# A fused attention and MLP kernel on one core: v's large part is loaded late, four waits are reordered, and the quotients are spread wider

## The chip, the cores and the metric

The kernel runs on one core of a Trainium2 chip. The metric is the device time of one execution in microseconds (us), the median of three runs. A profile of one execution goes with it. Engines are named as in the profile: PE multiplies matrices (PEld is its weight loading), DVE, ACT and POOL work element by element, SP issues the transfers (DMAs).

## The reference

There are 2048 tokens of 640 numbers each. One layernorm feeds two branches, and x is added to both:

```python
xn = layernorm(x)
return x + A(xn) + B(xn)

# A: linear attention, 32 heads of 20
q, k, v = split(xn @ wqkv)
phi(p) = concat(softmax(p @ w_phi), softmax(-(p @ w_phi)))   # per head, 20 -> 40 features
kv, z  = phi(k)^T v, sum over tokens of phi(k)
o      = phi(q) kv / (phi(q) z + 1e-6)                       # the quotient
A      = o @ wo

# B: MLP, 640 -> 1728 -> 640
B = gelu(xn @ w1 + b1) @ w2 + b2
```

## The kernel before, in words

Everything is float32. The kernel cuts each factor into a hi part, which PE's faster format holds exactly, and a lo part, the rest. Each product is three matmuls: hi by hi (line L70), hi by lo (L71), lo by hi (L72). Hi parts are cut by ACT (L61), lo parts by DVE or POOL (L64). PE's instructions are put in the order of the code by hand (`manual_schedule`). The other engines' orders come from a scheduler, which is held at some places by `issue_after`. Waits come from tiles and from the eight PSUM banks.

The work has three phases.

**Phase 1** (0 to 222 us) is the MLP for token blocks 0 and 1 (a block is 512 tokens). `mlp.passes(g, b)` takes two chunks of 128 hidden units: a first layer (`first`, then `gelu` at L260, then the split of the hidden tile m), and a second layer of five output pieces, each of which DVE adds to `acc` (L305). PE needs the bank that an L305 frees two pieces later. All that must be ready for phase 2 is made beside the MLP by the generator `prep()`, which is advanced once per three matmuls, about 0.68 us: the k and q weights are multiplied with `w_phi` (`prep_fold`: PE L460, then ACT L61 and DVE L64 out of the bank into `wkh` and `wkl`; a fold of q has two parts, so two hi and two lo), layernorm statistics, v's weights (`load_v`), and the normalised blocks 2 and 3 (`raw` is loaded, L532 on POOL subtracts, L535 on DVE multiplies, L539 on ACT and L542 on DVE split, and both parts go to DRAM). v's weights have a small part (128 columns), which goes into `wkh`/`wkl`, and a large part (512 columns), which is split in `prep()`, stored in DRAM as `wv_dram`, and read back at the start of phase 2 into the weight slots w2 and w3 (L584 to L588).

**Phase 2** (222.7 to 439 us) goes over 16 tiles of 128 tokens. `proj(t, i)` computes one of four column parts of a tile with 15 matmuls, i = 3 being v's large part. `k_tile` and `q_tile` make the features: maxima on DVE (L629, L630), differences on POOL (L640), the exponential on ACT (L641), sums on DVE (L643), quotients on POOL (L651, or L694 and L696). `kv_tile` multiplies k's features of a tile with its v, in ten matmuls L675 into banks that accumulate and one matmul L679 into the next bank in turn. `ptile` hands out banks 0, 1 and 2 in turn. `TAIL` lists the order of the last eight projections by hand.

**Phase 3** (439 to 731 us) is the MLP for blocks 2 and 3. Beside it run the last two `kv_tile`s (`last_kv`), and then `attend()`: for each block, groups of features are read from DRAM into `e`, split (ACT L893, POOL L894) and multiplied with kv (PE L900, L901), and `quotients()` divides (`ob`): it spreads the reciprocals `rx` over the partitions, one DVE shuffle (L944) and one POOL multiplication (L946) for each of five column chunks. At the end comes the output projection: `split` (L963, L965) and additions at L1068.

Of the kernel before, what the change touches and what calls it, by code (L numbers as in the profile page):

```python
# [15 lines left out]
P = 128  # L16
# [35 lines left out]
def tile_kernel(ctx: ExitStack, tc: tile.TileContext, x, xT, wkT, wqT, wv, wphi, wo, w1, b1, w2, b2,  # L52
# [33 lines left out]

    e_dram = [tc.dram_tile([2 * D, 512], F32, name=f"e{b}") for b in range(NB)]
    y_dram = [[tc.dram_tile([P, KC, 512], F32, name=f"y{p}{b}") for p in "hl"] for b in range(2)]
    wv_dram = [tc.dram_tile([P, KC, VF * H], F32, name=f"wv{p}") for p in "hl"]
    wo_dram = [tc.dram_tile([P, KC, D], F32, name=f"wo{p}") for p in "hl"]  # L90
    o_dram = [tc.dram_tile([2 * DH, 512], F32, name=f"o{b}") for b in range(NB)]
    r_dram = tc.dram_tile([2, 8, P], F32, name="r")
# [359 lines left out]
    def prep_fold(n, g, raw):  # L452

        kk, kd = (G6, G5) if g < 5 else (2 * DH, 2 * DF)
        parts = [(0, 0, DF)] if n == "k" else [(KQ, 0, B1F), (C3, B1F, DF)]

        for k, ni in ((0, 4), (4, 1)):
            ps = mlp.px()
            for i in range(ni):
                nc.tensor.matmul(ps[:, i * kd:(i + 1) * kd], raw[:kk, (k + i) * P:(k + i + 1) * P],  # L460
                                 wpt[:kk, g, :kd // DF, 1:], start=True, stop=True)
            for c, f0, f1 in parts:
                hi, lo = (w[:, k:k + ni, c:c + (f1 - f0) * H].rearrange("p i (f h) -> p i h f", h=H)[:, :, 6 * g:6 * g + kd // DF]
                          for w in wkv_)
                split(hi, lo, ps[:, :ni * kd].rearrange("p (i h f) -> p i h f", i=ni, f=DF)[:, :, :, f0:f1])
            for _ in range(3):
                yield

# [15 lines left out]
    def prep():  # L484
        jobs = [(n, g) for n in "kq" for g in range(6)]
        ahead = raws(*jobs[0])
        for _ in range(2):
            yield
        nc.vector.tensor_tensor(wpt[:, :, :, 1:], wpt[:, :, :, 1:], wpt[:, :, :, 0:1].to_broadcast([G6, 6, 6, DF]), op=ALU.subtract)
        more = more_stats()  # L490
        for i, job in enumerate(jobs):
            raw = ahead
            ahead = raws(*jobs[i + 1]) if i < 11 else None
            for k, _ in enumerate(prep_fold(*job, raw)):
                if i > 0 and k % 3 == 1:
                    next(more, None)
                yield

        def load_v(kc):
            raw = fp.tile([P, D], F32, name="raw")  # L500
            nc.sync.dma_start(raw, wv[kc * P:(kc + 1) * P, :])
            return raw

        for _ in more:
            yield
        ahead = load_v(0)
        mr = load_rows(2)
        for kc in range(KC):
            raw, ahead = ahead, load_v(kc + 1) if kc < KC - 1 else None
            for _ in range(5):  # L510
                yield
            split(*[w[:, kc, C2:C3] for w in wkv_], raw[:, VF * H:])
            t = fp.tile([P, 2, KC, G5], F32R, name="t").rearrange("p a c f -> p a (c f)")[:, :, :VF * H]
            split(t[:, 0], t[:, 1], raw[:, :VF * H])
            for p in range(2):
                nc.sync.dma_start(wv_dram[p][:, kc, :], f(t[:, p]))


        def load(b, c):
            xc = fp.tile([P, D], F32, name="raw")[:, :512]  # L520
            nc.sync.dma_start(xc, xT[c * P:(c + 1) * P, b * 512:(b + 1) * 512])
            return xc

        for b in range(2, 4):
            ahead = load(b, 0)
            if b == 3:
                mr = load_rows(3)
            for _ in range(5 if b == 2 else 10):
                yield
            for c in range(KC):  # L530
                xc, ahead = ahead, load(b, c + 1) if c < KC - 1 else None
                nc.gpsimd.tensor_tensor(xc, xc, mr[:, 0], op=ALU.subtract)  # L532
                for _ in range(3):
                    yield
                nc.vector.tensor_tensor(xc, xc, mr[:, 1], op=ALU.mult)  # L535
                for _ in range(2):
                    yield
                hl = fp.tile([P, 2, KC, G5], F32R, name="t").rearrange("p a c f -> p a (c f)")[:, :, :512]
                nc.scalar.activation(hl[:, 0], xc, AF.Copy)  # L539
                for _ in range(2):  # L540
                    yield
                nc.vector.tensor_tensor(hl[:, 1], xc, f(hl[:, 0]), op=ALU.subtract)  # L542
                for p in range(2):
                    nc.sync.dma_start(y_dram[b - 2][p][:, c, :], f(hl[:, p]))
                yield

    mlp.beside = prep()
    p11 = mlp.passes(1, 1, [wc[2], wc[3]])
    next(p11)
# [7 lines left out]
    for g in range(2, 7):  # L557
        for b in range(2):
            if b == 0:
                ws, wn = wn, []  # L560
            this = mlp.passes(g, b, ws)
            next(this)
            finish(before)
            before = this
            if g < 6:
                wn.append(mlp.take(2 * g + 2 + b))
            if 2 * g + b < 11:
                mlp.fetch(2 * g + 3 + b)
    finish(mlp.beside)
    finish(before)  # L570
    rs.close()
    order.close()
    for b in range(2):
# [9 lines left out]
    wv_ = [wp.tile([P, 4, D], F32R, name=f"w{2 + p}").rearrange("p i d -> p (i d)").rearrange("p (c d) -> p c d", c=KC)
           for p in range(2)]  # L584
    for p in range(2):
        nc.sync.dma_start(f(wv_[p]), wv_dram[p])
# [11 lines left out]
    def proj(t, i):  # L598
# [2 lines left out]
        c = slice((t % 4) * P, (t % 4) * P + P)  # L601
        wh, wl = [w[:, :, slice(*CB[i])] for w in wkv_] if i < 3 else wv_
        ps = ptile()[:, :wh.shape[2]]
        for kc in range(KC):
            mm3(ps, yh[:, kc, c], yl[:, kc, c], wh[:, kc], wl[:, kc], kc == 0, kc == KC - 1)
        return ps

    turn, exps, subs = [0], {}, {}
# [99 lines left out]
            nc.sync.dma_start(ed[q], ets[b][n][32 * q:32 * q + 32])  # L708

    fts, ets = {}, {}  # L710
    TAIL = [(14, 0), (14, 1), (15, 0), (15, 1), (14, 2), (14, 3), (15, 3), (15, 2)]
    places = [acc01.tile([P, KC, 512], F32, name=f"acc{n}").rearrange("p c (j n) -> p (c j) n", n=P) for n in range(2)]
    places = [p[:, j:j + 10] for p in places for j in (0, 10)] + [et.tile([P, 10, P], F32, name="et")]

# [1 line left out]
    for t, i in [(t, i) for t in range(14) for i in range(4)] + TAIL:  # L716
# [19 lines left out]
        else:  # L736
            evac = v_parts(t, ps, 0)

        tk = 13 if (t, i) == (15, 1) else t - 2 if 1 < t < 15 and i == 0 else None
        if tk is not None:  # L740
            kv_tile(tk, fts.pop(tk), vbuf[tk % 2])
        if i == 0 and t in (1, 2, 3, 6, 7):
# [7 lines left out]
            for w, wd in zip((f(hi), lo), wo_dram):  # L750
                nc.sync.dma_start(wd[:, kc, :], w)
        if (t, i) == (11, 0):
            mlp = Mlp((0, 2, 3, 1), ((1, 2), (0, 3)))
            mlp.ph = ptile
            mlp.fetch(0)
        if (t, i) == (12, 3):
# [93 lines left out]
    class Attention:  # L850
# [65 lines left out]
        def quotients(self):  # L916
# [25 lines left out]
            for c in range(KC + 1):  # L942
                if c < KC:
                    nc.vector.stream_shuffle(rx[:, c, :], rx[:, c, :], SPREAD)  # L944
                if c:
                    nc.gpsimd.tensor_tensor(ob[:, c - 1, :], ob[:, c - 1, :], rx[:, c - 1, :], op=ALU.mult)  # L946
# [185 lines left out]
```

## Time and profile before

| | us |
|---|---|
| three runs | 730.85, 732.10, 732.47 (median 732.1) |
| profiled execution | 732.27, its span 730.5 |
| PE busy | 719.0 (98% of the span), 3440 matmuls |
| DVE, POOL, ACT busy | 478.3, 371.3, 328.7 |

A row of the profile's timeline gives the start, the duration, the engine, the line of the kernel, the operation, the tiles it writes and reads, and in brackets how long the engine had been idle and what it waited for. The PE works almost without a break, so the question at each place is whether PE waits there and for whom. Idle time of another engine costs nothing in itself.

### The profile page before, as it was taken

To read this page: it belongs to the slowest core of one execution; us is meant where nothing else is said; L and a number is where in the kernel's file an instruction comes from. 1 tells how busy PE (TensorE), PEld (TensorE's weight loads), DVE (VectorE), ACT (ScalarE), POOL (GpSimd) and SP (SyncE) were. 2 spreads that over 40 slices of the span, in tenths; PEclk is the share of its full clock that TensorE was granted. 3 is DMA by queue.
4 is the path that set the end of the run, shared out by engine and by line. 5 is a ranking of instruction groups with operands and counts; after the bars stand their busy time and mean duration, and the time that the engine had idled before them with its cause. 6 is when DMAs were issued, how large, how long until landed. Compare 5 with 4: busy or idle time off the path is not lost.

```text
span 730.5 us, 9719 instructions
## 1 busy us (share of the span) xinstructions
PE 719.0 (98%) x3440; PEld 601.6 (82%) x3440; DVE 478.3 (65%) x796; ACT 328.7 (45%) x542; POOL 371.3 (51%) x322
## 2 busy tenths in 40 slices
PE   9999999999999999999999998999999999999998
PEld 7788878878888888888888887888878878887887
DVE  7837655466754788788898787435575656766431
ACT  7624554442423545545445546246565556530110
POOL 2211122234232997897878879346586777404000
PEclk9999999999999999999999999999999999999999
DMA  9704425754562127236302405934443453163222
GB/s 324 218 19 142 145 77 177 223 188 153 166 214 118 72 91 231 76 109 202 88 1 55 126 1 186 244 128 123 131 127 116 127 159 97 49 227 121 81 84 75
DMA packets 60016, 96.59 MB, mean 132 GB/s; under 512 B 7016, under 2 KB 28920, under 8 KB 58344
## 3 DMA queue, kind: packets, MB, share of 16 engines
q1 hardware_dynamic: 59680, 95.97, 42.0%
q8 instruction: 27, 0.44, 0.3%
q14 instruction: 21, 0.17, 0.1%
q10 hardware_dynamic: 288, 0.01, 0.0%
HBM read 65.61 MB, written 30.35 MB: 131 GB/s over the span
## 4 chain that ended last, share of the span: by engine, by line
PE 79%; DVE 8%; ACT 4%; DMA 3%; POOL 3%; issue 2%; SPq 0%; POOLq 0%; DVEq 0%; ACTq 0%
PE bank L70 24%; PE bank L71 23%; PE bank L72 23%; PE bank L675 2%; PE bank L460 2%; DVE rx L944 1%; DVE m L64 1%; POOL e L894 1%; PE bank L901 1%; DVE st L136 1%; PE bank L900 1%; DMA raw<-in_wv 1%; DVE y L965 1%; POOL w L64 1%; ACT m L260 1%
## 5 line engine op out<-in xcount | busy, mean ns | idle before, releaser
L64 POOL TENSOR_TENSOR w<-r,w 128x640 fp32r<-128x640 f32 x52 | 83.0, 1616 | 125.2 <-ACT w L61 96.0
L70 PE MATMUL bank<-y,w 128*128 128x512 f32 (+1 forms) x334 | 131.7, 394 | 0.4 <-DVE ob L1068 0.4
L71 PE MATMUL bank<-y,w 128*128 128x512 f32 (+1 forms) x334 | 129.9, 389 | 0.0
L72 PE MATMUL bank<-y,w 128*128 128x512 f32 (+1 forms) x334 | 129.8, 389 | 0.0
L70 PE MATMUL bank<-m,w 128*128 128x512 f32 x260 | 103.9, 400 | 3.5 <-DVE acc L305 2.5
L72 PE MATMUL bank<-m,w 128*128 128x512 f32 x260 | 101.5, 390 | 0.0
L71 PE MATMUL bank<-m,w 128*128 128x512 f32 x260 | 101.3, 390 | 0.0
L305 DVE TENSOR_TENSOR acc<-bank,acc 128x512 f32<-128x512 f32 x120 | 80.9, 683 | 16.8 <-PE bank L72 9.0
L70 PE MATMUL bank<-wkh,y 128*128 128x512 f32 (+1 forms) x240 | 87.7, 366 | 0.0
L71 PE MATMUL bank<-wkl,y 128*128 128x512 f32 (+1 forms) x240 | 87.4, 364 | 0.0
L72 PE MATMUL bank<-wkh,y 128*128 128x512 f32 (+1 forms) x240 | 87.0, 363 | 0.0
L64 DVE TENSOR_TENSOR m<-m,m 128x512 fp32r<-128x512 f32 (+1 forms) x54 | 42.6, 788 | 59.7 <-ACT m L61 59.7
L70 PEld LDWEIGHTS bank<-y,w 128*128 128x128 f32 x334 | 63.1, 189 | 13.4 <-DVE ob L1068 0.8
L72 PEld LDWEIGHTS bank<-y,w 128*128 128x128 f32 x334 | 63.2, 189 | 13.2
L71 PEld LDWEIGHTS bank<-y,w 128*128 128x128 f32 x334 | 63.2, 189 | 12.2
L641 ACT ACTIVATE m<-m,rs_all 128x1280 f32<-128x1280 f32 x32 | 43.7, 1365 | 42.6 <-POOL m L640 42.5
L70 PEld LDWEIGHTS bank<-m,w 128*128 128x128 f32 x260 | 48.9, 188 | 16.0 <-DVE acc L305 5.1
L643 DVE TENSOR_REDUCE sm<-m 128x64 f32<-128x1280 f32 x32 | 47.4, 1482 | 17.2 <-ACT m L641 17.0
L894 POOL TENSOR_TENSOR e<-e,m 128x512 fp32r<-128x512 f32 x28 | 38.1, 1361 | 40.1 <-ACT m L893 35.4
L72 PEld LDWEIGHTS bank<-m,w 128*128 128x128 f32 x260 | 48.8, 188 | 10.3
L71 PEld LDWEIGHTS bank<-m,w 128*128 128x128 f32 x260 | 48.9, 188 | 9.3
L260 ACT ACTIVATE m<-bank,b1t 128x512 f32<-128x512 f32 (+1 forms) x54 | 36.1, 670 | 44.7 <-PE bank L72 40.7
(156 smaller groups left out, 1395.5 us busy)
## 6 DMA issues: line engine op xcount, KB each, us to landing
r<-in_w SPq DMA_DIRECT2D x52, 320.0 KB
e<-e SPq DMA_DIRECT2D x40, 256.0 KB
e<-acc SPq DMA_DIRECT2D x52, 160.0 KB
acc<-in_xT SPq DMA_DIRECT2D x4, 1280.0 KB
xb<-in_x SPq DMA_DIRECT2D x8, 320.0 KB
t<-in_x SPq DMA_DIRECT2D x8, 320.0 KB
raw<-in_xT SPq DMA_DIRECT2D x10, 256.0 KB
yh<-t SPq DMA_DIRECT2D x10, 256.0 KB
```

The source lines that it names most:

```text
L64: eng.tensor_tensor(lo, src, f(hi), op=ALU.subtract)
L70: nc.tensor.matmul(ps, lh, rh, start=first, stop=False, **kw)
L71: nc.tensor.matmul(ps, lh, rl, start=False, stop=False, **kw)
L72: nc.tensor.matmul(ps, ll, rh, start=False, stop=last, **kw)
L136: nc.vector.bn_stats(st[:, i, h, :], xb[:, h * 320:(h + 1) * 320])
L260: nc.scalar.activation(gt, pz, AF.Gelu_apprx_tanh, bias=b1t[:, 2 * g + j:2 * g + j + 1])
L305: nc.vector.tensor_tensor(acc[b][:, m, :], pw, acc[b][:, m, :], op=ALU.add)
L460: nc.tensor.matmul(ps[:, i * kd:(i + 1) * kd], raw[:kk, (k + i) * P:(k + i + 1) * P], wpt[:kk, g, :kd // DF, 1:], start=True, stop=True)
L641: exps[n, t] = nc.scalar.activation(e, e, AF.Exp, scale=rs_all[:, t:t + 1])
L643: nc.vector.tensor_reduce(sm, e.rearrange("p s (h f) -> p (s h) f", f=DH), axis=AX, op=ALU.add)
L675: nc.tensor.matmul(kvp[g // 2][:, (g % 2) * 240:(g % 2) * 240 + 240].rearrange("p (s f) -> p s f", s=4), v[:, g * VS:(g + 1) * VS], ft[:, ...
L894: nc.gpsimd.tensor_tensor(pl, e, f(ph), op=ALU.subtract)
```

## The change

1. `wv_dram` is gone. `prep()` loads v's small part alone, with one strided DMA, and splits it once; eight steps of the generator stand where 25 stood. So the normalised blocks 2 and 3, which follow, are made 17 steps earlier. SP issues five loads of 320 KB, ten stores of 256 KB and two reads of 1280 KB less. The large part is loaded by `load_v` at pass (6, 0), five DMAs of 256 KB, and split by `split_v` straight into the slots w2 (hi, ACT) and w3 (lo, POOL) beside the second layer of that pass.
2. `prep_fold` issues both hi parts of a fold before both lo parts.
3. The last two projections change places: (15, 2) now comes before (15, 3). For i = 3, that is v's large part, in all 16 tiles, the five products hi by lo come first, then hi by hi and lo by hi in turn. `kv_tile(14)` comes right after (15, 3) and no longer inside the first layer of phase 3. The second MLP takes its weight slots in the order 0, 3, 2, 1, and `load_wo` uses w2 and w1.
4. `quotients()` leaves three steps between column chunks and no longer two.

```diff
@@ prep_fold
-            for c, f0, f1 in parts:
-                hi, lo = (w[:, k:k + ni, c:c + (f1 - f0) * H].rearrange("p i (f h) -> p i h f", h=H)[:, :, 6 * g:6 * g + kd // DF]
-                          for w in wkv_)
-                split(hi, lo, ps[:, :ni * kd].rearrange("p (i h f) -> p i h f", i=ni, f=DF)[:, :, :, f0:f1])
+            ops = [...]
+            for src, hi, lo in ops:
+                nc.scalar.activation(hi, src, AF.Copy)
+            for src, hi, lo in ops:
+                nc.vector.tensor_tensor(lo, src, f(hi), op=ALU.subtract)
@@ prep
-        ahead = load_v(0)
         mr = load_rows(2)
-        for kc in range(KC):
-            raw, ahead = ahead, load_v(kc + 1) if kc < KC - 1 else None
-            for _ in range(5):
-                yield
-            split(*[w[:, kc, C2:C3] for w in wkv_], raw[:, VF * H:])
-            t = fp.tile([P, 2, KC, G5], F32R, name="t").rearrange("p a c f -> p a (c f)")[:, :, :VF * H]
-            split(t[:, 0], t[:, 1], raw[:, :VF * H])
-            for p in range(2):
-                nc.sync.dma_start(wv_dram[p][:, kc, :], f(t[:, p]))
+        raw = fp.tile([P, D], F32, name="raw").rearrange("p (c d) -> p c d", c=KC)
+        nc.sync.dma_start(raw, wv[:, VF * H:].rearrange("(c p) d -> p c d", p=P))
+        for _ in range(8):
+            yield
+        split(*[w[:, :, C2:C3] for w in wkv_], raw)
+    def load_v():
+        raws = [fp.tile([P, 2, KC, G5], F32, name="t").rearrange("p a c f -> p (a c f)") for _ in range(2)]
+        raws = [raw[:, o:o + VF * H] for raw in raws for o in (0, VF * H)] + [fp.tile([P, D], F32, name="raw")[:, :VF * H]]
+        for kc, raw in enumerate(raws):
+            nc.sync.dma_start(raw, wv[kc * P:(kc + 1) * P, :VF * H])
+        return raws
+    def split_v():
+        for kc, raw in enumerate(raw_v):
+            split(wv_[0][:, kc], wv_[1][:, kc], raw, eng=nc.gpsimd)
+            yield
@@ the loop of phase 1
             next(this)
+            if (g, b) == (6, 1):
+                mlp.beside = split_v()
             finish(before)
             before = this
+            if (g, b) == (6, 0):
+                finish(mlp.beside)
+                raw_v = load_v()
+                wv_ = [... w2 and w3 ...]
@@ proj
-        for kc in range(KC):
-            mm3(ps, yh[:, kc, c], yl[:, kc, c], wh[:, kc], wl[:, kc], kc == 0, kc == KC - 1)
+        ops = [(lh, rh, kc) for kc in range(KC) for lh, rh in ((yh, wh), (yh, wl), (yl, wh))]
+        if i == 3:
+            ops.sort(key=lambda op: op[1] is wh)
+        for n, (lh, rh, kc) in enumerate(ops):
+            nc.tensor.matmul(ps, lh[:, kc, c], rh[:, kc], start=n == 0, stop=n == 3 * KC - 1)
@@ the end of phase 2
-    TAIL = [(14, 0), (14, 1), (15, 0), (15, 1), (14, 2), (14, 3), (15, 3), (15, 2)]
+    TAIL = [(14, 0), (14, 1), (15, 0), (15, 1), (14, 2), (14, 3), (15, 2), (15, 3)]
-        tk = 13 if (t, i) == (15, 1) else t - 2 if 1 < t < 15 and i == 0 else None
+        tk = {(15, 1): 13, (15, 3): 14}[t, i] if (t, i) in ((15, 1), (15, 3)) else t - 2 if 1 < t < 15 and i == 0 else None
-            mlp = Mlp((0, 2, 3, 1), ((1, 2), (0, 3)))
+            mlp = Mlp((0, 3, 2, 1), ((1, 2), (0, 3)))
@@ last_kv
-        for t in (14, 15):
-            for _ in range(1 if t == 14 else 9):
-                yield
-            kv_tile(t, fts[t], vbuf[t % 2])
+        for _ in range(10):
+            yield
+        kv_tile(15, fts[15], vbuf[1])
@@ quotients
-                for i in range(2):
+                for i in range(3):
                     yield
@@ load_wo
-            w = wp.tile([P, 4, D], F32R, name=f"w{(3, 1)[p]}")
+            w = wp.tile([P, 4, D], F32R, name=f"w{(2, 1)[p]}")
```

The first place where the order of instructions matters is ACT, early in phase 1, when q's folds begin. The name before `<-` is the tile written; m4 is the hidden tile that the gelu writes, wkh the folds' hi part, and the brackets name the engine that the instruction waits for. Before:

```order
L61 ACTIVATE wkh_616<-bank3_984 128x4x6x13 [waits PE_49]
L61 ACTIVATE wkh_616<-bank3_984 128x4x6x6 [waits DVE_49]
L260 ACTIVATE m4_958<-bank2_960,b1t_60 128x512 [waits Activation_49]
L61 ACTIVATE m0_959<-m4_958 128x512 [waits Activation_49]
L61 ACTIVATE wkh_616<-bank4_1010 128x6x13 [waits PE_49]
L61 ACTIVATE wkh_616<-bank4_1010 128x6x6 [waits DVE_49]
```

After (the lines are numbered anew, L465 is the fold's hi part and L259 the gelu):

```order
L465 ACTIVATE wkh_614<-bank3_982 128x4x6x13 [waits PE_49]
L465 ACTIVATE wkh_614<-bank3_982 128x4x6x6
L259 ACTIVATE m4_956<-bank2_958,b1t_60 128x512 [waits DVE_49]
L61 ACTIVATE m0_957<-m4_956 128x512 [waits Activation_49]
L465 ACTIVATE wkh_614<-bank4_1008 128x6x13 [waits PE_49]
L465 ACTIVATE wkh_614<-bank4_1008 128x6x6
```

ACT's instructions stand in the same sequence. The second hi part of a fold waited for DVE's first lo part and does not any more.

The second place is PE where phase 2 ends. `w1_3957` holds the features of tile 15 and `v1` its v; `y01_3061` is block 3 and `w0` the first weights of the MLP. Before, the end of the tile's L675 and L679, and the first layer for block 3 behind them:

```order
L675 MATMUL bank6_2017<-w1_3957,v1_2036 128x240 x2
L675 MATMUL bank7_2018<-w1_3957,v1_2036 128x240 x2
L679 MATMUL bank0_4186<-w1_3957,v1_2036 128x160
L70 MATMUL bank1_4212<-y01_3061,w0_3716 128x512
L71 MATMUL bank1_4212<-y11_3062,w0_3716 128x512
```

After, the same place (L689 and L693 are the two lines of `kv_tile`):

```order
L689 MATMUL bank6_1994<-w1_3930,v1_2009 128x240 x2
L689 MATMUL bank7_1995<-w1_3930,v1_2009 128x240 x2
L693 MATMUL bank0_4159<-w1_3930,v1_2009 128x160
L70 MATMUL bank1_4185<-y01_3034,w0_3689 128x512
L71 MATMUL bank1_4185<-y11_3035,w0_3689 128x512
```

The rows read alike, but the banks have other histories. Before, bank 0 held the first hidden chunk of phase 3 (`bank0_4124`, freed by its gelu) and bank 1 tile 14's L679. Now bank 0 held tile 14's L693 (`bank0_4077`) and bank 1 the first hidden chunk (`bank1_4110`). So the matmul that waits for the first gelu of phase 3 is L70 of the next first layer, one place later than L679.

The third place is POOL at about 580 to 591 us, where quotients (L946, and L959 after) lie between lo parts of features (L894, and L907 after; `e_5263` and `e_5236` are the same tile). Before:

```order
L946 TENSOR_TENSOR ob1_4736<-ob1_4736,rx_4369 128x512 x2
L894 TENSOR_TENSOR e_5207<-e_5207,m5_4379 128x512
L946 TENSOR_TENSOR ob1_4736<-ob1_4736,rx_4369 128x512
L64 TENSOR_TENSOR w3_5322<-r1_5184,w3_5322 128x640
L64 TENSOR_TENSOR w3_5322<-r2_5185,w3_5322 128x640
L946 TENSOR_TENSOR ob1_4736<-ob1_4736,rx_4369 128x512
L894 TENSOR_TENSOR e_5237<-e_5237,m5_4379 128x512
L946 TENSOR_TENSOR ob1_4736<-ob1_4736,rx_4369 128x512
L894 TENSOR_TENSOR e_5263<-e_5263,ph_4380 128x512
```

After:

```order
L959 TENSOR_TENSOR ob1_4709<-ob1_4709,rx_4342 128x512
L907 TENSOR_TENSOR e_5180<-e_5180,m5_4352 128x512
L959 TENSOR_TENSOR ob1_4709<-ob1_4709,rx_4342 128x512
L64 TENSOR_TENSOR w2_5293<-r1_5157,w2_5293 128x640
L64 TENSOR_TENSOR w2_5293<-r2_5158,w2_5293 128x640
L907 TENSOR_TENSOR e_5210<-e_5210,m5_4352 128x512
L959 TENSOR_TENSOR ob1_4709<-ob1_4709,rx_4342 128x512 x2
L907 TENSOR_TENSOR e_5236<-e_5236,ph_4353 128x512
L959 TENSOR_TENSOR ob1_4709<-ob1_4709,rx_4342 128x512
```

One of the five quotients that stood ahead of that tile's lo part now stands behind it.

More of the change, by code (lines that the diff above doesn't have):

```diff
@@ L88, in tile_kernel @@
     y_dram = [[tc.dram_tile([P, KC, 512], F32, name=f"y{p}{b}") for p in "hl"] for b in range(2)]
-    wv_dram = [tc.dram_tile([P, KC, VF * H], F32, name=f"wv{p}") for p in "hl"]
     wo_dram = [tc.dram_tile([P, KC, D], F32, name=f"wo{p}") for p in "hl"]
@@ L461, in prep_fold @@
                                  wpt[:kk, g, :kd // DF, 1:], start=True, stop=True)
-            for c, f0, f1 in parts:
-                hi, lo = (w[:, k:k + ni, c:c + (f1 - f0) * H].rearrange("p i (f h) -> p i h f", h=H)[:, :, 6 * g:6 * g + kd // DF]
-                          for w in wkv_)
-                split(hi, lo, ps[:, :ni * kd].rearrange("p (i h f) -> p i h f", i=ni, f=DF)[:, :, :, f0:f1])
+            ops = [(ps[:, :ni * kd].rearrange("p (i h f) -> p i h f", i=ni, f=DF)[:, :, :, f0:f1],
+                    *(w[:, k:k + ni, c:c + (f1 - f0) * H].rearrange("p i (f h) -> p i h f", h=H)[:, :, 6 * g:6 * g + kd // DF]
+                      for w in wkv_)) for c, f0, f1 in parts]
+            for src, hi, lo in ops:
+                nc.scalar.activation(hi, src, AF.Copy)
+            for src, hi, lo in ops:
+                nc.vector.tensor_tensor(lo, src, f(hi), op=ALU.subtract)
             for _ in range(3):
@@ L497, in prep @@
                 yield
[L499 to L502, printed above, removed]
         for _ in more:
             yield
-        ahead = load_v(0)
         mr = load_rows(2)
-        for kc in range(KC):
-            raw, ahead = ahead, load_v(kc + 1) if kc < KC - 1 else None
-            for _ in range(5):
-                yield
-            split(*[w[:, kc, C2:C3] for w in wkv_], raw[:, VF * H:])
-            t = fp.tile([P, 2, KC, G5], F32R, name="t").rearrange("p a c f -> p a (c f)")[:, :, :VF * H]
-            split(t[:, 0], t[:, 1], raw[:, :VF * H])
-            for p in range(2):
-                nc.sync.dma_start(wv_dram[p][:, kc, :], f(t[:, p]))
+        raw = fp.tile([P, D], F32, name="raw").rearrange("p (c d) -> p c d", c=KC)
[3 more added lines that the diff above has]
+        split(*[w[:, :, C2:C3] for w in wkv_], raw)
         def load(b, c):
@@ L562, in tile_kernel @@
             next(this)
+            if (g, b) == (6, 1):
+                mlp.beside = split_v()
             finish(before)
             before = this
+            if (g, b) == (6, 0):
+                finish(mlp.beside)
+                raw_v = load_v()
+                wv_ = [wp.tile([P, 4, D], F32R, name=f"w{2 + p}").rearrange("p i d -> p (i d)").rearrange("p (c d) -> p c d", c=KC)
+                       for p in range(2)]
             if g < 6:
@@ L568, in tile_kernel @@
                 mlp.fetch(2 * g + 3 + b)
+    finish(before)
     finish(mlp.beside)
-    finish(before)
     rs.close()
@@ L582, in tile_kernel @@
     a = ExitStack()
[L583 to L586, printed above, removed]
     vp = a.enter_context(tc.tile_pool(name="vA", bufs=1, reuse_waits="tile"))
```

## The prediction

> **What bounds the kernel now.** I read the page's busy times first, then what PE waits for, then PE's own timeline around each wait, and last the engine that each wait names.
>
> ```profile
> span 730.5 us, 9719 instructions
> PE 719.0 (98%) x3440; PEld 601.6 (82%) x3440; DVE 478.3 (65%) x796; ACT 328.7 (45%) x542; POOL 371.3 (51%) x322
> ```
>
> PE is busy for 98% of the span, and the change removes no matmul. So it can gain only PE's waits, and they are short (engine, tile and line, what was waited for: us in total, times, longest):
>
> ```profile
> PE bank L70 <- DVE acc L305: 2.5, 3, 1.3
> PE bank L679 <- ACT m L260: 1.9, 1, 1.9
> PE bank L901 <- POOL e L894: 0.6, 1, 0.6
> PE bank L70 <- DVE ob L1068: 0.4, 1, 0.4
> ```
>
> What a wait costs is more than its length, and the timeline shows by how much (start, duration, engine, line, operation, tiles, idle before):
>
> ```profile
> 446.58 0.39 PE L71 MATMUL bank<-y,w 128*128 128x512 f32 x1
> 446.81 0.40 PE L72 MATMUL bank<-y,w 128*128 128x512 f32 x1
> ...
> 102.03 0.50 PE L70 MATMUL bank<-m,w 128*128 128x512 f32 x1 [1.02 <-DVE acc L305]
> 102.37 0.40 PE L71 MATMUL bank<-m,w 128*128 128x512 f32 x1
> ```
>
> Matmuls of 512 columns start 0.23 us apart but last 0.39: each is still in the pipeline for 0.16 us when the next one starts. A wait empties it, so its gap costs 0.16 more than it shows; and the first matmul behind it holds its successor off for 0.34, which is 0.11 more. **A wait costs its gap and 0.27.** One wait costs more still:
>
> ```profile
> 450.20 0.36 PE L679 MATMUL bank<-w,v 128*128 128x160 f32 x1 [1.87 <-ACT m L260]
> ...
> 450.86 0.63 PE L71 MATMUL bank<-y,w 128*128 128x512 f32 x1
> 451.28 0.63 PE L72 MATMUL bank<-y,w 128*128 128x512 f32 x1
> ```
>
> Behind it the matmuls start 0.42 apart, and a table by stretches shows why (us from the span's start, length, the five engines' busy times, granted clock, DMA share, GB/s):
>
> ```profile
> 446.90:450.30 3.40, 1.53 (x13) 1.29 (x11) 2.12 (x3) 3.37 (x4) 3.40 (x5) 1.00 1.05 395
> 450.40:453.80 3.40, 3.40 (x9) 2.67 (x9) 3.15 (x9) 3.40 (x8) 3.08 (x6) 0.50 0.22 83
> ```
>
> The granted clock is 0.50 for the 3.4 us behind the wait, 1.00 before. Eight matmuls at 0.42 instead of 0.23 lose about 1.6 us. This wait therefore costs 1.87 + 0.27 + 1.6 = 3.74 us, the most of all.
>
> **The change part by part.** *Folds of q, the wait at 102 us.* ACT and DVE stand in the chain before it:
>
> ```profile
> 94.93 0.44 ACT L61 ACTIVATE wkh<-bank 128x144 fp32r<-128x144 f32 x1 [0.83 <-DVE wkl L64]
> ...
> 97.59 0.24 ACT L61 ACTIVATE wkh<-bank 128x36 fp32r<-128x36 f32 x1 [0.92 <-DVE wkl L64]
> ...
> 101.29 0.68 DVE L305 TENSOR_TENSOR acc<-bank,acc 128x512 f32<-128x512 f32 x1
> ```
>
> ACT stops before the second hi part of a fold until DVE has cut the first lo part, 0.83 and 0.92 us here, with gelu and the hidden tile's split queued behind it. In the new order this wait is gone; DVE's first lo part starts one short ACT operation later instead (0.24 to 0.44 us). ACT gains at least the two waits, 1.75 us. PE waited 1.02 for the L305 that is last in this chain, so that L305 must come 1.02 earlier, and 1.75 − 0.44 = 1.31 are to be had. I take the wait as gone: gain 1.02 + 0.27 = **1.29**. Ends: 0 (DVE is the limit after all), 1.29; nearer to 1.29, since ACT's waits are direct.
>
> *y-part 17 steps earlier, the wait at 148.8 us.*
>
> ```profile
> 142.88 1.29 POOL L532 TENSOR_TENSOR raw<-raw,m 128x512 f32<-128x512 f32 x1 [2.03 <-DMA raw<-in_xT]
> 144.20 0.69 DVE L535 TENSOR_TENSOR raw<-raw,m 128x512 f32<-128x512 f32 x1 [2.09 <-POOL raw L532]
> 144.93 0.63 ACT L539 ACTIVATE t<-raw 128x512 fp32r<-128x512 f32 x1 [3.54 <-DVE raw L535]
> 148.05 1.28 DVE L305 TENSOR_TENSOR acc<-bank,acc 128x512 f32<-128x512 f32 x2
> 148.79 0.50 PE L70 MATMUL bank<-m,w 128*128 128x512 f32 x1 [1.31 <-DVE acc L305]
> 149.36 0.39 PE L72 MATMUL bank<-m,w 128*128 128x512 f32 x1
> 149.59 0.40 PE L70 MATMUL bank<-m,w 128*128 128x512 f32 x1
> ```
>
> A late load makes POOL late, POOL makes DVE late by 2.09, DVE makes ACT late by 3.54, ACT's gelu waits behind the L539 that waits, and the second layer's L305 comes late. Seventeen steps of 0.68 us put this piece 11.6 us earlier, beside another pass, and ahead of the loads SP issues five loads and ten stores less. Its 1.31 + 0.27 = **1.58** are gone there. What is late next is the same chain at its new place. Its bounds are 0 and 1.58 (again); I take 0: of the three waits for L305 above, one is at 102, one at 624 and only one here, so nine of the ten pieces of this kind are hidden.
>
> *v's large part.* Its splits are five ACT and five POOL operations beside pass (6, 0), at about 213 to 220 us. POOL's cover there is this row's idle time:
>
> ```profile
> 230.10 1.28 POOL L640 TENSOR_TENSOR m<-m,mx 128x640 f32<-128x640 f32 x1 [11.27 <-DVE mx L629]
> ```
>
> POOL stands idle until 230.10 for 11.27 us; five splits of 128x512 at 1.29 (L532's duration) are 6.5. The lo parts are first read by the fourth projection of phase 2, behind three of 15 matmuls that begin at 222.7, so after 229 us: some 9 us to spare. The five loads are issued a pass earlier. Cost 0. If the cover were gone, PE would wait for what is left of 6.5 us; half of it, 3.2, is my bound. The two reads of 1280 KB that went before are gone and were hidden too.
>
> *The end of phase 2, the wait at 450 us.* It waits for gelu of the first hidden chunk, and that stands behind tile 15's q features on ACT:
>
> ```profile
> 440.31 1.57 POOL L64 TENSOR_TENSOR w<-r,w 128x640 fp32r<-128x640 f32 x1
> 442.59 1.42 POOL L640 TENSOR_TENSOR m<-m,mx 128x600 f32<-128x600 f32 x2 [0.71 <-DVE mx L629]
> ...
> 446.78 1.36 ACT L641 ACTIVATE m<-m,rs_all 128x1280 f32<-128x1280 f32 x1 [3.81 <-POOL m L640]
> 448.16 1.28 ACT L260 ACT_TABLE_LOAD   x1
> 449.46 0.69 ACT L260 ACTIVATE m<-bank,b1t 128x512 f32<-128x512 f32 x1
> ```
>
> With (15, 2) ahead of (15, 3) its projection ends 15 matmuls of 0.23, so 3.4 us, earlier, and so do its maxima. But POOL is busy with the split of a weight until 441.87 (its order is unchanged), and only its 0.71 us of waiting for the maxima disappears. Then come the same differences, exponential, table load and gelu: gelu ends at 449.44 and not 450.15. L679 of tile 15 no longer waits; L70 behind it does. The gap becomes 1.87 − 0.71 = 1.16. Whether the clock halves is decided between 1.31, the gap at 148.79 above, behind which the matmuls keep their 0.23, and 1.87. 1.16 lies below both, so I take no drop. Cost 1.16 + 0.27 = 1.43 where 3.74 was: gain **2.31**. Ends: 0.71 (clock halves again), and 3.74 (chain shorter than I follow it).
>
> [...]
>
> *kv_tile(14), slots.* Its eleven matmuls run earlier, their inputs long made, and their number is the same: 0. The slots only rename tiles.
>
> *Lo products first, 16 projections of 15 matmuls.* The three products no longer stand side by side, so fewer neighbours share the stationary y.
>
> ```profile
> L71 PE MATMUL bank<-y,w 128*128 128x512 f32 (+1 forms) x334 | 129.9, 389 | 0.0
> L72 PE MATMUL bank<-y,w 128*128 128x512 f32 (+1 forms) x334 | 129.8, 389 | 0.0
> L71 PEld LDWEIGHTS bank<-y,w 128*128 128x128 f32 x334 | 63.2, 189 | 12.2
> ```
>
> L71 has the same stationary factor as L70 ahead of it, L72 has not, and both take 389 ns; L71 loads its weights like all others (189 ns, below the spacing of 230). Cost 0.
>
> *Quotients three steps apart.* The waits left in phase 3:
>
> ```profile
> 546.03 0.39 PE L72 MATMUL bank<-m,w 128*128 128x512 f32 x1
> 546.54 0.50 PE L70 MATMUL bank<-m,w 128*128 128x512 f32 x1
> ...
> 624.51 0.50 PE L70 MATMUL bank<-m,w 128*128 128x512 f32 x1 [0.16 <-DVE acc L305]
> ...
> 584.97 1.30 POOL L946 TENSOR_TENSOR ob<-ob,rx 128x512 f32<-128x512 f32 x1
> 620.10 0.75 DVE L944 STREAM_SHUFFLE rx<-rx 128x512 f32<-128x512 f32 x1
> ```
>
> At 546.54 (gap 0.12) DVE has shuffles of 0.75 ahead of its L305, and fewer of them stand there after: 0.12 + 0.27 = 0.39 gained. The wait of 0.6 for POOL's L894: one L946 of 1.30 moves behind it, so it goes: 0.87. At 624.51: 0.16 + 0.27 = 0.43; DVE is relieved, but its lo part waits for POOL there, so I take 0.33. The wait of 0.4 for L1068: one shuffle of 0.7 fewer ahead of it, 0.67. Sum **2.26**. Ends: 2.36, and −1.0, should a moved shuffle or multiplication put an L305 or L894 of a later row behind as long as the longest of these four (0.87) did.
>
> **The sum.** 1.29 + 1.58 + 2.31 + 2.26 = 7.44 us. The profiled execution took 732.27 us, within 0.2 us of the median of 732.1: 732.27 − 7.44 = 724.8.
>
> **The rivals.**
>
> *The clock halves again.* If POOL's or DVE's part in the chain is no shorter, gelu is at most 0.71 earlier or not at all, and with the half clock behind it the term of 2.31 becomes 0 to 0.71: 732.27 − 7.44 + 2.31 = 727.1 with 0. For it: a gap between 1.31 and 1.87 would do, and 1.16 is only 0.15 below. Against it: 0.71 is read straight from POOL's row.
>
> *Phase 1 gives part back.* The folds' lo parts now come later on DVE, and the y-part runs beside the folds' end and other loads. A new wait like those at 102 or 148.8 costs 1.3 to 1.6; one or both leave 726.1 to 727.7. For it: L532 was late there because of a load, and that load must still come in time. Against it: ACT only loses waits, and SP has fifteen transfers fewer.
>
> *The half clock is not the wait's.* The slow stretch then stays whatever the gap is, and 1.6 of the gain is lost: 726.4. Against it: it begins where the longest wait ends. [...]
>
> *Slower, by the lo-first order.* If two neighbours with the same stationary factor do run faster than two with different ones, 240 matmuls lose it. It decides from (1.46 + 7.44) / 240 = 37 ns each, 16% of their spacing; at 50 ns it gives 732.3 − 7.4 + 12 = 737. Against it: the two rows of 389 and the weight load for each matmul. A milder form, 10 ns, is 2.4 us and 727.2.
>
> *The waits only move.* PE loses at the next place what it gains at one, because DVE, ACT or POOL have the same work to do in phase 1 and 3: about 732. For it: POOL's and DVE's operations are only reordered. Against it: each wait was the end of a chain with idle time in it, ACT's 0.92 and DVE's 2.09, and those go.
>
> **How the numbers follow.** A measurement of this kernel tells about 0.2%, 1.46 us, from no change (its three runs lie 1.6 us apart). My forecast, from 723.2 to 726.2, has 0.57; the clock 0.14; phase 1 0.12; the half clock on its own 0.04; slower by the order 0.05; waits that only move 0.08. So faster 0.87 (all but the last two), less 0.01 for 10 ns with another rival on top: 0.86; same 0.08; slower 0.06. The range goes down to 723.0, 7.44 and the rest of the wait at 450 (1.43) and some, and up to 728.8, the clock rival with one wait of 1.6 in phase 1. It leaves out 0.17.
>
> **What would show it.** In the profile after: no wait of PE for L305 around 100 and in 130 to 150 us; no wait of ACT's second hi part; PE's wait for gelu at about 445 us shorter than 1.3 us, on L70, with a granted clock of 1.0 behind it; POOL's differences of tile 15's q directly behind L64; no wait for L894 at about 585 and none above 0.3 for L305 and L1068 behind 540; the sixteen projections of v's large part with the same 0.23 between matmuls; PE not waiting for w3 at 225 to 232. The prediction is wrong if the half clock shows again, if L305 or L532 appear with new waits, or if PE waits for v's lo part.

## The result, and the profile after

The changed kernel takes 724.36 us (median of four runs, 724.30 to 724.48); the kernel before took 732.06 with the run beside it (730.85 to 732.47). The ratio is 0.9898, with a 95% interval of 0.9881 to 0.9915: 7.7 us or 1.0% faster. Forecast were 724.8 us, 723.0 to 728.8. In all comparisons an execution that ran at a lower clock from end to end is left out; this concerns one of the runs below (889.5 us, clock 0.753).

The head of the page after, its first two lines:

```profile
span 722.7 us, 9696 instructions
...
PE 715.3 (99%) x3440; PEld 600.7 (83%) x3440; DVE 473.5 (66%) x787; ACT 327.3 (45%) x538; POOL 376.3 (52%) x327
```

PE's 3440 matmuls are still there, and the span is 7.8 us shorter. What PE waits for now (all groups of the view):

```profile
PE bank L373 <- POOL m L371: 1.3, 1, 1.3
PE bank L70 <- ACT m L259: 1.0, 1, 1.0
PE bank L70 <- DVE acc L302: 0.9, 2, 0.6
PE bank L178 <- DVE xb L169: 0.6, 2, 0.4
```

Of the seven waits that the prediction priced, six are gone: both L305 waits of phase 1 and all four behind 540 us. One is left, that for the first gelu of phase 3. The three other groups lie in the first 75 us. The kernel before has them too, two of them shorter and another of 0.2 us beside them. PE's timeline at the wait that is left, with a table by stretches of 3.4 us (columns as in the prediction):

```profile
445.36 0.24 PE L693 MATMUL bank<-w,v 128*128 128x160 f32 x1
446.59 0.50 PE L70 MATMUL bank<-y,w 128*128 128x512 f32 x1 [1.00 <-ACT m L259]
446.92 0.40 PE L71 MATMUL bank<-y,w 128*128 128x512 f32 x1
447.16 0.39 PE L72 MATMUL bank<-y,w 128*128 128x512 f32 x1
```

```profile
442.40:445.80 3.40, 3.19 (x20) 2.70 (x18) 1.23 (x1) 2.61 (x2) 3.40 (x4) 1.00 0.69 257
445.80:449.20 3.40, 2.61 (x11) 2.18 (x12) 2.22 (x5) 3.36 (x7) 3.40 (x6) 1.00 0.27 93
449.20:452.60 3.40, 3.40 (x16) 2.82 (x15) 3.40 (x8) 1.73 (x4) 3.37 (x5) 1.00 0.33 98
```

L693 of tile 15 no longer waits, and L70 behind it waits 1.00 us where 1.16 was forecast. The granted clock stays 1.00, and the matmuls keep 0.24.

Both timelines have 3440 matmuls, so the n-th of the one can be set beside the n-th of the other. At 99 us the two are level. From there the kernel before falls behind by 1.31 us at 102, 1.45 at 149, 2.57 at 450 and 2.65 in phase 3 (at the four waits and at 544.3, where a matmul is held up without a wait in the list, 0.17): 7.97 in all with rounding. Between these places the distance moves by no more than 0.04. Behind the last matmul the changed kernel takes 0.17 us longer (3.70 against 3.53), so the spans differ by 7.8. The profiled executions differ by 732.27 − 724.48 = 7.79. So the whole difference lies in these places, and PE loses at no later place what it gains at one.

### The profile page after: what moved, and what is told of

The parts are those of the page before. It is cut to its first block, busy times and chain, and to the rows that moved or that the text cites. A ratio compares the mean times of both kernels' runs of the same rounds, so it can differ in the third digit from the quotient of the medians.

```text
span 722.7 us, 9696 instructions
## 1 busy us (share of the span) xinstructions
PE 715.3 (99%) x3440; PEld 600.7 (83%) x3440; DVE 473.5 (66%) x787; ACT 327.3 (45%) x538; POOL 376.3 (52%) x327
## 4 chain that ended last, share of the span: by engine, by line
PE 87%; DVE 5%; POOL 2%; ACT 2%; issue 1%; DMA 1%; SPq 0%; POOLq 0%; ACTq 0%
PE bank L619 23%; PE bank L70 18%; PE bank L72 18%; PE bank L71 18%; PE bank L459 2%; PE bank L689 2%; POOL m L654 2%; PE bank L913 1%; PE bank L914 1%; DVE st L135 1%; POOL m L665 1%; PE bank L300 1%; PE bank L281 1%; PE bank L280 1%; PE bank L299 1%
## 5 line engine op out<-in xcount | busy, mean ns | idle before, releaser
L619 PE MATMUL bank<-wkh,y 128*128 128x512 f32 (+1 forms) x480 | 139.5, 364 | 0.0
L70 PE MATMUL bank<-y,w 128*128 128x512 f32 (+1 forms) x334 | 130.8, 392 | 1.0 <-ACT m L259 1.0
L70 PE MATMUL bank<-m,w 128*128 128x512 f32 x260 | 103.4, 398 | 1.0 <-DVE acc L302 0.9
L619 PEld LDWEIGHTS bank<-wkh,y 128*128 128x128 f32 x480 | 87.5, 188 | 13.3
L304 DVE TENSOR_TENSOR acc<-bank,acc 128x512 f32<-128x512 f32 x120 | 81.1, 684 | 21.7 <-PE bank L72 14.1
L70 PEld LDWEIGHTS bank<-y,w 128*128 128x128 f32 x334 | 62.8, 188 | 13.5 <-ACT m L259 1.2
L259 ACT ACTIVATE m<-bank,b1t 128x512 f32<-128x512 f32 (+1 forms) x54 | 36.2, 671 | 53.3 <-PE bank L72 48.5
L70 PEld LDWEIGHTS bank<-m,w 128*128 128x128 f32 x260 | 48.9, 188 | 11.8 <-DVE acc L302 1.1
L907 POOL TENSOR_TENSOR e<-e,m 128x512 fp32r<-128x512 f32 x28 | 36.3, 1296 | 41.8 <-ACT m L906 33.7
L72 PEld LDWEIGHTS bank<-m,w 128*128 128x128 f32 x260 | 48.8, 188 | 10.4
L619 PE MATMUL bank<-w,y 128*128 128x512 f32 x240 | 57.4, 391 | 0.0
```

The lines of the kernel that those rows point to most:

```text
L70: nc.tensor.matmul(ps, lh, rh, start=first, stop=False, **kw)
L72: nc.tensor.matmul(ps, ll, rh, start=False, stop=last, **kw)
L259: nc.scalar.activation(gt, pz, AF.Gelu_apprx_tanh, bias=b1t[:, 2 * g + j:2 * g + j + 1])
L304: nc.vector.tensor_tensor(acc[b][:, m, :], pw, acc[b][:, m, :], op=ALU.add)
L619: nc.tensor.matmul(ps, lh[:, kc, c], rh[:, kc], start=n == 0, stop=n == 3 * KC - 1)
L907: nc.gpsimd.tensor_tensor(pl, e, f(ph), op=ALU.subtract)
```

## The experiments

Every kernel below is the changed kernel (724.36 us) with the edit shown. Each has four to six runs, beside the kernel before.

**Folds: lo part right behind its hi part.**

```diff
             for src, hi, lo in ops:
                 nc.scalar.activation(hi, src, AF.Copy)
-            for src, hi, lo in ops:
                 nc.vector.tensor_tensor(lo, src, f(hi), op=ALU.subtract)
```

> The changed kernel (724.4 us), with each lo part of a fold right behind its hi part again. My theory: ACT's wait before each second hi part returns, and with it PE's wait of about 1 us for the L305 near 100 us, so 1.3 us more: 725.7. Rival: that wait went because of something else in phase 1 (v's part gone), and the order of the split is worth nothing: 724.4.

725.69 us (725.59 to 726.11), 1.33 more. ACT of this kernel, and then the same stretch of the changed kernel:

```profile
95.21 0.44 ACT L465 ACTIVATE wkh<-bank 128x144 fp32r<-128x144 f32 x1 [0.83 <-DVE wkl L466]
...
97.87 0.24 ACT L465 ACTIVATE wkh<-bank 128x36 fp32r<-128x36 f32 x1 [0.92 <-DVE wkl L466]
```

```profile
94.38 0.39 ACT L465 ACTIVATE wkh<-bank 128x78 fp32r<-128x78 f32 x2 [0.17 <-PE bank L459]
...
97.34 1.02 ACT L465 ACTIVATE wkh<-bank 128x312 fp32r<-128x312 f32 x2 [0.21 <-PE bank L459]
```

ACT's 0.83 and 0.92 are back to the hundredth, and PE waits 0.97 us for L305 (L304 there) at 102. In the changed kernel both hi parts stand as one group of two, and wait for PE alone.

**Quotients: two steps apart.**

```diff
-                for i in range(3):
+                for i in range(2):
```

> The changed kernel with two steps between column chunks of the quotients and not three. My theory: the four waits behind 540 us return (DVE's L305 twice, POOL's lo part of a feature tile, DVE's addition in the output projection), 0.39 + 0.87 + 0.43 + 0.64 = 2.3 us more: 726.7. Rival: they went because tiles and slots of phase 3 changed (weight slots 0, 3, 2, 1) or because the phase starts elsewhere: 724.4.

727.06 us (726.78 to 727.22), 2.70 more. Its waits of PE, without the groups that the changed kernel has as well:

```profile
PE bank L178 <- DVE xb L169: 1.1, 2, 0.7
...
PE bank L914 <- POOL e L907: 0.6, 1, 0.6
PE bank L70 <- DVE ob L1081: 0.4, 1, 0.4
...
PE bank L70 <- DVE acc L304: 0.2, 1, 0.2
```

The waits for POOL's lo part, for the output projection's L1081 and for L304 return, and so does the gap of 0.12 at 541. Set beside the changed kernel matmul by matmul, this one falls behind by 2.63 us at these places, among them 0.16 at 539.0, which the theory had left out. The first line is a wait in the first 20 us, which the edit can't reach: it puts this profile 0.24 us behind, and from 150 us on less than 0.1 of that is left.

**v's products side by side.**

```diff
-        if i == 3:
-            ops.sort(key=lambda op: op[1] is wh)
```

> The changed kernel with the three products of v's large part side by side again (hi by hi, hi by lo, lo by hi), nothing else edited. Theory: the order costs nothing per matmul (0.227 us between matmuls either way), but it sets when the slot w3 is free: with lo products first after 5 matmuls of (15, 3), with the old order at its end. ACT's and POOL's split of the first-layer weights into w3 then comes later, behind the differences of tile 15's q on POOL (the instruction order has moved so), gelu comes 1.5 us earlier and PE's wait for it goes (1.26 us less), but PE waits for w3's lo part instead, from 441.3 to about 443.2, 1.9 + 0.27, with 1.8 more if the clock halves: 725.2 to 727.1. Rival 1: the order is of no account, 724.4. Rival 2: neighbours with the same stationary factor are faster, 240 matmuls gain 10 ns or more each: 722 or less, and the spacing in v's projections shows it.

725.13 us (725.06 to 725.20), 0.77 more, just under the range of the first theory. First the price of a matmul in v's projections, this kernel and the changed one (total busy, mean ns):

```profile
L616 PE MATMUL bank<-w,y 128*128 128x512 f32 x240 | 57.4, 391 | 0.0
```

```profile
L619 PE MATMUL bank<-w,y 128*128 128x512 f32 x240 | 57.4, 391 | 0.0
```

These durations have modelled ends, so the starts count for more: set side by side, the two kernels keep their distance of 0.15 us from 170 to 430 us, through the projections of v's large part of fourteen tiles. The order is worth nothing per matmul. That it is worth something at the end of phase 2, PE and POOL show (this kernel):

```profile
440.90 0.39 PE L71 MATMUL bank<-y,w 128*128 128x512 f32 x1
442.99 0.51 PE L72 MATMUL bank<-y,w 128*128 128x512 f32 x1 [1.70 <-POOL w L64]
```

```profile
438.77 2.67 POOL L651 TENSOR_TENSOR m<-mx,m 128x600 f32<-128x600 f32 x2
441.41 1.53 POOL L64 TENSOR_TENSOR w<-r,w 128x640 fp32r<-128x640 f32 x1
```

POOL of the changed kernel, where the differences are L654:

```profile
437.55 1.58 POOL L64 TENSOR_TENSOR w<-r,w 128x640 fp32r<-128x640 f32 x1
439.09 2.66 POOL L654 TENSOR_TENSOR m<-m,mx 128x600 f32<-128x600 f32 x2
```

The split into w3 stands behind the differences now, PE waits 1.70 us for it, and the wait for gelu is gone: 1.70 + 0.27 − (1.00 + 0.27) = 0.7. The clock stayed at 1.0 in all five runs. Lo products first are what frees w3 after five matmuls of (15, 3), early enough for POOL.

**The end of phase 2 as before,** with `kv_tile(14)` and `load_wo`'s slots as before, too.

```diff
-    TAIL = [..., (14, 2), (14, 3), (15, 2), (15, 3)]
+    TAIL = [..., (14, 2), (14, 3), (15, 3), (15, 2)]
-            mlp = Mlp((0, 3, 2, 1), ((1, 2), (0, 3)))
+            mlp = Mlp((0, 2, 3, 1), ((1, 2), (0, 3)))
```

> The changed kernel with the end of phase 2 as before: (15, 3) ahead of (15, 2), the eleven matmuls of tile 14 inside the first layer, weight slots 0, 2, 3, 1; lo products first is kept. My theory: PE's wait for gelu returns at 1.87 us with the half clock behind it, 2.7 us more: 727.1; an execution whose clock windows lie otherwise may keep the full clock, then 1.84 less, 725.3. Rival: the clock's slow stretch belongs to something else and stays away: 725.3 in every run with a wait of 1.87. Rival 2: it moves nothing, 724.4.

Five runs: 725.36, 725.73, 726.85, 726.89, 726.99, median 726.85, 2.49 more. The first two had a mean granted clock of 0.999, the others 0.997. The profiled one (725.36) has the old wait and no slow stretch behind it:

```profile
447.33 0.34 PE L693 MATMUL bank<-w,v 128*128 128x160 f32 x1 [1.88 <-ACT m L259]
447.51 0.44 PE L70 MATMUL bank<-y,w 128*128 128x512 f32 x1
447.78 0.39 PE L71 MATMUL bank<-y,w 128*128 128x512 f32 x1
448.01 0.39 PE L72 MATMUL bank<-y,w 128*128 128x512 f32 x1
```

So the same wait is followed by half clock in some executions and not in others. The kernel before does the same: of the 29 runs made beside these experiments 12 had a mean clock of 0.997 or 0.998, with a median of 732.15 us, and 17 had 0.999 or 1.000, with a median of 730.46. Set beside the profile of the kernel before, which has the half clock behind its wait of 1.87, this one gains 1.59 us across the place: that is what the half clock cost there.

**A copy on ACT ahead of gelu's table load, 512 or 1024 columns wide.**

```diff
+    idle = mtile(5).rearrange("p s f -> p (s f)")[:, :512]
     with tc.issue_after(exps["q", 15].ins):
+        nc.scalar.activation(idle, f(y[2][0]).rearrange("p c t -> p (c t)")[:, :512], AF.Copy)
         next(before)
```

> The changed kernel with one copy of 128x512 that nothing reads on ACT, between the exponential of tile 15's q and the table load for gelu (0.53 to 0.63 us). Theory: ACT is in the chain to gelu, so PE's wait grows by as much, from 1.0 to 1.55, and the time by 0.55: 724.9 in every run, the clock at 1.0 (kernels with a wait of 1.70 kept it in 6 of 6 runs). Rival: there is slack between ACT and gelu: 724.4. Rival 2: the clock halves already at 1.55 in some runs: 726.7 in those.

> As the one before with a copy of 128x1024 (1.05 to 1.15 us). Theory: PE's wait grows to 2.1 us, the time by 1.1 to 725.5 in the runs whose clock stays, and 1.84 more, 727.3, in those where half clock follows; with 1.87 us it followed in 11 of 18 runs, so here in about two thirds of them. [...] Rival: above some length it halves always: all runs at 727.3. Rival 2: it never halves: 725.5 in all.

With 512 columns: 724.93 us (724.87 to 724.97), 0.57 more, a wait of 1.52 us, the clock at 0.999 or 1.0 in all four runs. ACT is in the chain without slack. (The expectation counts six runs with a wait of 1.70; there are five.) With 1024 columns: 725.15, 725.41, 725.65 with a clock of 0.999 or 1.0, and 726.96, 727.30 with 0.997. The profile is of the last:

```profile
447.77 0.50 PE L70 MATMUL bank<-y,w 128*128 128x512 f32 x1 [1.96 <-ACT m L259]
448.11 0.57 PE L71 MATMUL bank<-y,w 128*128 128x512 f32 x1
448.47 0.63 PE L72 MATMUL bank<-y,w 128*128 128x512 f32 x1
```

```profile
444.76:448.17 3.41, 1.45 (x12) 1.25 (x11) 3.33 (x6) 3.38 (x5) 3.11 (x6) 1.00 0.36 106
448.17:451.58 3.41, 3.41 (x10) 2.67 (x9) 2.59 (x7) 3.41 (x8) 3.15 (x4) 0.50 0.16 27
```

Half clock begins at 448.17 and not when PE resumes at 447.77. Counted back by its own length, 3.41 us, the stretch ahead of it holds the wait whole, 445.82 to 447.77, and PE was busy for 1.45 us of it. In the kernel before the slow stretch began at 450.39, and the stretch from 446.98 held its wait whole as well (448.33 to 450.20), with PE busy for 1.54 us. In the profiled execution of the kernel with the old end of phase 2 the clock stayed at 1.00 through its wait of 1.88 and behind it:

```profile
442.73:446.14 3.41, 2.72 (x18) 2.25 (x16) 0.83 (x1) 2.21 (x2) 3.41 (x4) 1.00 1.05 399
446.14:449.55 3.41, 2.22 (x10) 1.88 (x11) 3.16 (x7) 3.40 (x7) 3.10 (x7) 1.00 0.77 278
```

The trace gives the times at which the clock changed. In the kernel before, full clock is first recorded at 6.66 us; it changes 443.733, 447.146 and 723.626 us after that, which is 130, 131 and 212 times 3.4133 us. In the changed kernel it is first recorded at 5.48 us and changes once, 716.799 us (210 times) after that. The last change of each comes when PE has ended its work. Around the waits of 1.70 (v's products side by side) and of 1.52 (512 columns) the clock stayed at 1.00, too:

```profile
440.56:443.98 3.42, 1.72 (x8) 1.11 (x7) 1.88 (x2) 2.49 (x2) 3.42 (x3) 1.00 0.87 331
444.02:447.43 3.41, 1.89 (x15) 1.65 (x14) 2.55 (x3) 3.35 (x5) 3.41 (x6) 1.00 0.44 139
```

So of the profiles two have half clock, behind waits of 1.87 and 1.96 us, and those with waits of 1.88, 1.70 and 1.52 have full clock. Of the runs of the two kernels with waits of 1.87 and 1.88, 15 of 34, 44%, had it; waits of 1.70 and 1.52 never brought it, in nine runs. What decides it in one execution, the clock windows that an expectation above names or something else, was not shown: no run set by hand where the wait lies.

**y-pieces late, v's part as changed.**

```diff
-        for _ in range(8):
+        for _ in range(25):
             yield
         split(*[w[:, :, C2:C3] for w in wkv_], raw)
```

> The changed kernel with 25 idle steps instead of 8 ahead of the split of v's small part, so that the normalised blocks 2 and 3 come as late as before the change, but v's large part is still loaded late and nothing of it goes through DRAM. Theory: the place of the y-pieces beside the passes made the wait of 1.31 us near 148; it returns, 1.3 to 1.6 us more: 725.7 to 726.0. Rival: the transfers of v's large part (five loads, ten stores) made that load late; they stay away, so no wait returns: 724.4.

724.42 us (724.28 to 724.87): the theory fell. The y-pieces stand at their old place beside the passes (the first load is issued at 136.24 us; in the kernel before, which is 1.3 us behind by then, at 137.91), and PE has no wait there. The 17 steps are not needed to take the wait away. Whether they would have been enough with v still going through DRAM, no run shows.

**v through DRAM again, and then one transfer moved in SP's queue.** The first kernel has all of v's part undone (the old loop in `prep()`, `wv_dram`, the reads into w2 and w3). The second differs from it in this alone (`xload[0]` is the load of the first y-piece):

```diff
-            raw, ahead = ahead, load_v(kc + 1) if kc < KC - 1 else None
+            raw, ahead = ahead, load_v(kc + 1) if kc < KC - 1 else load(2, 0)
...
-            for p in range(2):
-                nc.sync.dma_start(wv_dram[p][:, kc, :], f(t[:, p]))
+            with tc.issue_after(xload[0].ins) if xload else ExitStack():
+                for p in range(2):
+                    nc.sync.dma_start(wv_dram[p][:, kc, :], f(t[:, p]))
```

> The changed kernel with its first part undone as a whole: v's five row blocks are loaded in prep(), both parts of the large part go to DRAM (ten stores) and are read back at the start of phase 2. Theory, after the run with the late y-pieces alone kept 724.4: not the place of the y-pieces but v's loads, splits and stores ahead of them made the wait of 1.31 us; with them it returns: 1.3 to 1.6 us more, 725.7 to 726.0. Rival: the wait needed the other wait of phase 1 (at 102 us) too, and stays away: 724.4.

> As the one before (v through DRAM), but one order of SP's queue is changed: the load of the first y-piece stands ahead of the stores of v's last row block, not behind the first of them, which waits for ACT's split; it is to be issued 2 to 2.6 us earlier. All transfers, splits and buffers are the same. Theory: the load was late because SP's queue stood behind that store; the wait near 148 goes: 724.4. Rival: the load is slow because 16 DMA engines are 83% busy with v's stores and weights, or the engines' work for v is what delays the chain; the wait stays: 725.7 to 726.0.

v through DRAM: 725.89 us (724.89 to 726.25), 1.53 more, and PE waits again for L305:

```profile
PE bank L70 <- DVE acc L305: 1.2, 1, 1.2
```

With the load first: 724.15 us (724.09 to 724.62), and the wait is gone, though every store, split and buffer is there. SP's queue of the one and of the other (start, time until issued):

```profile
132.76 3.20 SPq L519 DMA_DIRECT2D wvh<-t  x2
136.05 0.38 SPq L519 DMA_DIRECT2D wvl<-t  x1
136.49 0.45 SPq L524 DMA_DIRECT2D raw<-in_xT  x1
```

```profile
133.20 0.32 SPq L527 DMA_DIRECT2D wvl<-t  x1
133.61 0.41 SPq L511 DMA_DIRECT2D raw<-in_xT  x1
135.36 0.32 SPq L527 DMA_DIRECT2D wvh<-t  x1
```

In the first kernel the load is issued 2.9 us later, behind a store that waited for ACT's split of v's last row block. What follows from it, POOL and ACT of the first kernel, then of the second:

```profile
141.55 1.28 POOL L535 TENSOR_TENSOR raw<-raw,m 128x512 f32<-128x512 f32 x1 [2.13 <-DMA raw<-in_xT]
...
143.59 0.63 ACT L542 ACTIVATE t<-raw 128x512 fp32r<-128x512 f32 x1 [3.46 <-DVE raw L538]
```

```profile
139.08 1.29 POOL L538 TENSOR_TENSOR raw<-raw,m 128x512 f32<-128x512 f32 x1
...
141.56 0.63 ACT L545 ACTIVATE t<-raw 128x512 fp32r<-128x512 f32 x1 [1.51 <-DVE raw L541]
```

POOL starts 2.5 us earlier without a wait for the transfer, ACT 2.0 us earlier.

**The lo part of w3 on DVE, and then with a load moved.** The split on POOL that stands in the chain to gelu goes to DVE (the new argument is the engine of its lo part); the second kernel also holds `store_phi(3, ...)` in SP's queue behind the load of chunk 3's second half.

```diff
-            w, late = mlp.take_parts(1)
+            w, late = mlp.take_parts(1, nc.vector)
```

> The changed kernel, with the lo part of the second chunk's first-layer weights (the split into w3 at the end of phase 2) cut by DVE and not by POOL. Theory: that split of 1.58 us on POOL stands in the chain to gelu (POOL differences of tile 15's q, exponential, table load, gelu); without it gelu ends 1.5 us earlier, PE's last wait of 1.0 us there is gone with its 0.27: 723.1. Rival: the chain is held by DVE's maxima or by ACT, so gelu stays: 724.4; DVE has the work now, and if its lo part comes late, PE waits for w3 instead: 724.4 or more.

> The kernel with w3's lo part on DVE (723.9), and the stores of the last features of q held in SP's queue behind the load of the second half of chunk 3's weights. Theory: its new wait of PE (0.40 us for DVE at 462.5) came from that load, issued 3 us late behind stores that wait for transposes, over ACT's split and DVE's; with the load first the wait goes: 723.2 to 723.4, the fastest so far. Rival: the stores, later now, delay the reading of these features, or DVE is late by its own work: 723.9 or more.

The first takes 723.90 us (723.38 to 724.16). Gelu's wait is gone: POOL's 1.58 us were in the chain. But PE has a new wait of 0.40 us for DVE, at 462.9. ACT's split of weights waits for a load, and SP issued that load behind two stores that waited for transposes (SP, ACT, and PE's wait):

```profile
452.84 1.88 SPq L722 DMA_DIRECT2D e<-acc  x2
454.82 0.40 SPq L222 DMA_DIRECT2D r<-in_w  x1
```

```profile
458.33 0.74 ACT L61 ACTIVATE w<-r 128x640 fp32r<-128x640 f32 x1 [3.85 <-DMA r<-in_w]
```

```profile
PE bank L859 <- DVE km L838: 0.4, 1, 0.4
```

The second takes 723.46 us (723.29 to 723.88; ratio to before 0.9898, 0.9882 to 0.9914), just above the range of its theory, and the view of waits lists none of PE's between 75 us and the end. Set side by side, the two profiles part by 0.68 us at the wait that went, its 0.40 and 0.27; their runs overlap. It is the fastest here; none of its runs is as slow as the fastest of the changed kernel.

## Why the prediction was right, and where it was not

| step | forecast us | matmul by matmul | undone, medians |
|---|---|---|---|
| folds | 1.29 | 1.31 | 1.33 |
| wait at 148.8 | 1.58 | 1.45 | 1.53 |
| wait at 450 | 2.31 | 2.57 | 2.49 |
| quotients | 2.26 | 2.65 | 2.70 |
| lo products first | 0 | 0 per matmul | 0.77 |
| sum | 7.44 | 7.97 | |

- *What a wait costs.* Its gap and 0.27 held to within 0.03 us (1.31 for 1.02 at 102), as did the reading that only PE's waits can be gained. The rivals by which phase 1 gives part back or the waits only move fall: between these places the two kernels keep their distance.
- *Folds.* Right in mechanism and size.
- *The wait at 148.8.* Right in size (0.12 of it is left at 146.0, too little to be listed as a wait), wrong in cause. The step that failed is "Seventeen steps of 0.68 us put this piece 11.6 us earlier": they aren't needed. The chain of four engines that the prediction quoted is real, but its head was not the transfer's place in the program; it was SP's queue, where the load waited behind a store. The prediction named the fifteen transfers that go and gave them no price.
- *The wait at 450.* The mechanism was right: POOL's split in the chain, the wait 0.71 shorter by forecast and 0.87 by measurement, the clock up. Those 0.16 us are the larger part of what the term lacks (2.31 against 2.57). The half clock was sized right: 1.6 us forecast, 1.59 between two profiles with the same wait, and 1.59 again between those of the two copies on ACT once the 0.44 by which their waits differ is taken off; the 1.84 in some expectations is too much. Missed was that half clock follows this wait in fewer than half of the executions (15 of 34). The medians shown happened to have it; against executions of the kernel before without it (730.46) the gain is 6.1 and not 7.7 us. The rival by which the clock halves again allowed a gap between 1.31 and 1.87; one of 1.70 kept the clock, and 1.00 was far off. The rival that the half clock is not the wait's falls too: a longer wait alone, by the copy of 1024 columns, brought it back in two of five runs, and in the two profiles that show it, it begins 0.19 and 0.40 us behind the end of such a wait.
- *Lo products first.* Its price per matmul, 0, is right, and the rival "slower by the order" falls, with 391 ns on both sides and the starts level. The step was incomplete: the order also frees w3 early, and "POOL is busy with the split of a weight until 441.87 (its order is unchanged)" holds only because of it.
- *Quotients.* All four waits went. The term was too small by 0.39: 0.17 came at 544.3, which was not priced, 0.46 at 624.5 where 0.33 was taken, and the rest in hundredths.
- *v's large part at no cost.* Right: POOL's five splits ran from 212.3 to 218.6 and the zeroing of v to 221.3, ahead of its next work at 227.4, and PE has no wait for w3 there.

## What to carry to other kernels

When PE is busy for 98%, list its waits, price each as gap plus the refilling of its pipeline (0.27 us here), and check behind each long one whether the granted clock fell (to 0.50 here, behind 1.87 and 1.96 us). Follow each wait back to the head of its chain, and read the issuing queue there too: a load that is late may only stand behind a store that waits for an engine, and moving that one transfer was worth as much as taking fifteen away (724.15 us and 724.36). An order of equal matmuls cost nothing by itself here (391 ns each either way), but it decided when an operand's buffer was free for what came next.

## What was not expected of the hardware

- A wait of 1.87 to 1.96 us was followed by half clock (for 3.41 us in the two profiles that show it, 1.59 us lost) in 17 of 39 executions, and one of 1.52 or 1.70 in none of nine. So the kernel before has two times, 730.5 and 732.2 us, and a median of few runs falls on either. The four runs of the changed kernel lie within 0.2 us.
- The clock changed only at whole multiples of 3.4133 us after full clock was first recorded: 130, 131 and 212 times in the profile of the kernel before, 210 times in that of the changed one. Half clock began not at the end of the wait but later, 0.19 us after PE resumed in the kernel before and 0.40 with the copy of 1024 columns.
